# Attention on one core: the own weights u·r·k as stationary columns beside another tile's logits, and a matmul with ones in place of a transposition

## The chip, the core and the metric

The kernel runs on one core of a Trainium2 chip. The metric is the device time of one execution in microseconds (us), as a median over runs. The core has a matrix engine (TensorE, PE in the rows, with PEld for its weight loads), VectorE (DVE), ScalarE (ACT), GpSimd (POOL), and SyncE (SP), which issues most DMA transfers. TensorE multiplies a stationary operand, which is loaded into its array column by column, with a moving operand that streams through; results go to PSUM. A matmul with fp32 operands is issued as two passes, each with a weight load of its own, so four such matmuls stand in a row as x8.

## The reference

A linear attention over 768 steps (batch 4, 8 heads of width 48) feeds two mixture-of-experts layers. Only the attention and the logits of the first gate matter here:

```
for t in range(S):
    cur = einsum('bhd,bhe->bhde', u * kt, vt)
    y[:, :, t] = einsum('bhd,bhde->bhe', rt, state + cur)
    state = w * state + einsum('bhd,bhe->bhde', kt, vt)
...
x = y.transpose(0, 2, 1, 3).reshape(B * S, H * D)      # 3072 tokens of width 384
logits = x @ w_gate ; eom = sigmoid(x @ w_output_gate)
```

The term with `cur` gives a token its own value: for each head, y gets (sum over d of u·r·k) times v. This one number for each token and head is called its own weight here.

## The kernel before

The tokens are cut into 24 tiles of 128 (6 chunks of time for 4 batches). A loop over t = 0 to 23 runs the attention as a pipeline: in iteration t each step works on the tile that it is ready for. The order in which the instructions of TensorE, VectorE and ScalarE stand is the order of the code, written out by hand; each engine works through its list in order. The steps, by their names in the code and in the rows:

- `s_rk` (VectorE): `rks`, r and k of tile t+1 times powers of w. `s_pr` (GpSimd): `rkp`, the product r·k of tile t+1. `s_kn` (GpSimd): `kn`.
- `s_a` (TensorE): `a`, the products of r and k inside tile t, 8 matmuls; `s_am` (VectorE) masks them into `am`. Two PSUM banks hold `a`, so the next tile's `a` needs this tile's `am`.
- `s_t` (TensorE): 4 transpositions of tile t-2's output into the bank `t`. `s_csm` (TensorE) puts the own weights of tile t into spare columns of that bank: 4 matmuls with `rkp` stationary (128 columns) and `usel` moving (two columns, u of the two heads of a pair). In the first two iterations there is no `s_t`, and the bank is called `c`.
- `s_cs` (VectorE) copies the own weights out as `cs`; `s_cv` (ScalarE) multiplies v by them, 8 small activations, `cv`, one iteration later; `s_x` (VectorE) adds `cv` to the transposed output: `x`.
- `s_y` (TensorE): `y` of tile t-1, from the state (`st`) and from `am`; `s_yt` (ScalarE) copies it out.
- `s_l` (TensorE): the logits of tile t-4, 3 matmuls with the gate's weights `wg_s` stationary (32 columns) and the transposed tokens `xth` moving. Each of the three parts of the width 384 goes into a group of 32 PSUM partitions of its own in the bank `sp`; the fourth group is unused. `s_s` puts the update of the state into the same bank.
- `s_xt` (TensorE) and `s_xh` (ScalarE): transposition of the tokens of tile t-3 into `xth`.
- `s_ls` (ScalarE) copies the 96 partitions of logits out, `s_lt` (TensorE) transposes them into the bank `lg` of their group of tiles, and `s_r1` (VectorE) adds the three parts and starts the routing; `s_r2`, `s_r3`, `s_r4` finish it, and GpSimd scatters the tokens to their experts (`xs`). For the last groups a matmul with `fold` (ones that add the three parts) takes the place of the transposition already.

After the loop a hand-written tail finishes tiles 20 to 23. In its last steps six scatters run on GpSimd, one behind the other. Then 26 warm-up matmuls run on TensorE, and the first expert stage begins with loads of the scattered tokens (`xe<-xs`).

At the start `usel` is made by two copies on VectorE. In iteration 2 a check of w (`s_flag`) computes `okr` on VectorE and a matmul of it on TensorE.

## Time and profile before

| what | value |
|---|---|
| median of 3 runs | 1927.33 us (1926.3 to 1927.76) |
| the profiled execution's own time | 1927.44 us |
| its span, from the first to the last instruction | 1925.4 us |
| TensorE busy over the span | 98% |
| VectorE, ScalarE, GpSimd busy | 70%, 43%, 24% |
| granted TensorE clock, mean | 0.987 |
| iteration 4 of the attention loop begins | 42.59 us |
| its tail begins | 160.34 us |

The times in the rows count from the first instruction of the span. A busy TensorE is one that has a matmul under way; matmuls overlap, so what a step costs is read from the start of its first matmul to the start of the next step's first matmul. The clock is given as a share of its upper level of 2.4 GHz; 0.50 is the lower level of 1.2 GHz.

### The profile page before, as it was taken

The page shows a single profiled execution, that of the slowest core. Times are in us where ns is not written, and L with a number is a line of the kernel's source. Part 1 is how long each engine was busy: PE and PEld are TensorE (multiplying, and loading weights), DVE is VectorE, ACT ScalarE, POOL GpSimd, SP SyncE. Part 2 cuts the span into 40 slices and gives each one's busy share as a digit, 9 for nine tenths or more (in the row PEclk, how much of TensorE's full clock was granted, in tenths as well). Part 3 has the DMA queues.
Part 4 walks back from the last instruction along what each step waited for, and adds up shares of the span by engine and source line. Part 5 has one row for each costly group of instructions (what it writes and reads, how often), then busy time and mean ns, then how long its engine had stood idle before and what let it go on. Part 6 is the DMA issues. An engine that isn't in the chain of part 4 may idle for free.

```text
span 1925.4 us, 27928 instructions
## 1 busy us (share of the span) xinstructions
PE 1890.4 (98%) x10851; PEld 1715.8 (89%) x10852; DVE 1347.9 (70%) x2296; ACT 834.2 (43%) x1687; POOL 471.0 (24%) x507
## 2 busy tenths in 40 slices
PE   8998999999999999999999999999999999999998
PEld 6886999977989999999999888999999999999997
DVE  6885555666887677777777787567777777667774
ACT  2664444444444444434444444543443444444432
POOL 4673000211213322221111344122111111111112
PEclk7998999999999999999999999999999999999999
DMA  7764444221111111111111112111111111111101
GB/s 223 238 209 127 139 129 135 73 59 34 34 34 34 33 34 34 34 41 41 34 33 34 33 33 78 38 34 34 33 39 37 34 33 37 39 33 34 33 25 49
DMA packets 43916, 118.39 MB, mean 61 GB/s; under 512 B 6737, under 2 KB 10065, under 8 KB 43777
## 3 DMA queue, kind: packets, MB, share of 16 engines
q1 hardware_dynamic: 38944, 107.04, 19.4%
q0 software_dynamic: 3904, 9.47, 1.4%
q8 instruction: 86, 1.41, 0.3%
q14 instruction: 54, 0.43, 0.1%
q10 hardware_dynamic: 928, 0.04, 0.0%
HBM read 101.96 MB, written 14.56 MB: 61 GB/s over the span
## 4 chain that ended last, share of the span: by engine, by line
PE 73%; DVE 2%; issue 2%; POOL 1%; ACT 0%; POOLq 0%; DVEq 0%
PE o L1217 39%; PE bS L1170 13%; PE bT L1170 11%; PE bZ L1170 4%; PE bW L1170 4%; POOL out L1237 1%; DVE wal L875 1%; POOL ws L846 1%; DVE hc L1183 0%; PE lgp L1097 0%; DVE hl L1204 0%; DVE slot L925 0%; DVE x L1235 0%; ACT hc L1180 0%; PE pcp L1146 0%
## 5 line engine op out<-in xcount | busy, mean ns | idle before, releaser
L1217 PE MATMUL o<-wbh,hl 128*128 128x384 f32 x1536 | 518.6, 338 | 0.4 <-DVE hl L1204 0.3
L1217 PE MATMUL o<-wbl,hh 128*128 128x384 f32 x1536 | 518.5, 338 | 0.0
L1217 PE MATMUL o<-wbh,hh 128*128 128x384 f32 x1536 | 517.5, 337 | 0.7 <-DVE x L1229 0.3
L846 POOL TENSOR_TENSOR ws<-ra 128x384 f32<-128x384 f32 (+2 forms) x192 | 195.0, 1044 | 1093.1 <-DVE wal L875 1013.6
L1204 DVE SCALAR_TENSOR_TENSOR hl<-hc,hh 128x512 fp32r<-128x512 f32 x384 | 278.3, 727 | 206.7 <-ACT hh L1203 201.1
L1217 PEld LDWEIGHTS o<-wbh,hh 128*128 128x128 f32 x1536 | 289.1, 188 | 42.7 <-DVE x L1235 1.1
L1217 PEld LDWEIGHTS o<-wbh,hl 128*128 128x128 f32 x1536 | 288.3, 188 | 43.1 <-DVE hl L1204 1.3
L1217 PEld LDWEIGHTS o<-wbl,hh 128*128 128x128 f32 x1536 | 288.5, 188 | 0.0
L1180 ACT COPY hc<-bT 128x512 f32<-128x512 f32 x192 | 113.0, 588 | 400.4 <-PE bT L1170 398.6
L1180 ACT COPY hc<-bS 128x512 f32<-128x512 f32 x192 | 112.9, 588 | 370.8 <-PE bS L1170 370.7
L1203 ACT ACTIVATE hh<-hc 128x512 fp32r<-128x512 f32 x384 | 240.1, 633 | 11.7 <-PE o L1217 11.7
L1170 PE MATMUL bS<-slot,wah 128*128 128x512 f32 x704 | 226.0, 394 | 8.7 <-DVE hc L1183 6.6
L1235 DVE SCALAR_TENSOR_TENSOR x<-o,pw,x 128x384 f32<-128x384 f32 x348 | 204.9, 610 | 22.3 <-PE o L1217 17.9
L1170 PE MATMUL bT<-slot,wah 128*128 128x512 f32 x640 | 201.1, 396 | 0.0
L1183 DVE TENSOR_TENSOR hc<-bS,hc 128x512 f32<-128x512 f32 x192 | 132.2, 688 | 43.2 <-PE bS L1170 41.6
L1170 PE MATMUL bS<-slot,wal 128*128 128x512 f32 x384 | 151.6, 395 | 0.0
L1170 PEld LDWEIGHTS bS<-slot,wah 128*128 128x128 f32 x704 | 128.5, 188 | 15.3 <-DVE hc L1183 9.7
L875 DVE TENSOR_TENSOR wal<-ws,wah 128x384 fp32r<-128x384 f32 (+2 forms) x192 | 133.1, 693 | 9.3 <-ACT wah L874 9.2
L1170 PE MATMUL bT<-slot,wal 128*128 128x512 f32 x320 | 126.3, 395 | 0.0
L1183 DVE TENSOR_TENSOR hc<-bT,hc 128x512 f32<-128x512 f32 x128 | 87.9, 687 | 52.5 <-PE bT L1170 49.8
L874 ACT CAST wah<-ws 128x384 fp32r<-128x384 f32 (+2 forms) x192 | 117.6, 612 | 3.0 <-POOL ws L846 3.0
L1170 PEld LDWEIGHTS bT<-slot,wah 128*128 128x128 f32 x640 | 116.5, 188 | 2.4 <-DVE hc L1189 0.8
(235 smaller groups left out, 2705.1 us busy)
## 6 DMA issues: line engine op xcount, KB each, us to landing
raw<-in_wm SPq DMA_DIRECT2D x64, 384.0 KB
ra<-in_wm SPq DMA_DIRECT2D x64, 384.0 KB
rb<-in_wm SPq DMA_DIRECT2D x64, 384.0 KB
rk<-in_rkt SPq DMA_DIRECT2D x25, 448.0 KB
na<-in_nat SPq DMA_DIRECT2D x25, 384.0 KB
xs<-zer SPq DMA_DIRECT2D x8, 624.0 KB
xe<-xs SPq DMA_DIRECT2D x8, 624.0 KB
xs<-x,posl POOLq DMA_INDIRECT x24
```

The costliest lines, as they stand in the source:

```text
L846: gsum.append(tc.keep_in_program_order(nc.gpsimd.tensor_tensor(*x)))
L874: nc.scalar.copy(hi[:, q], x)
L875: nc.vector.tensor_tensor(lo[:, q], x, hi[:, q].bitcast(F32), ALU.subtract)
L1170: nc.tensor.matmul(bank[bk], w_[:, at, :], x_, start=(opens == 1 and n == 0), stop=(n == 2), skip_group_check=True)
L1180: A.copy(hid(u, *copy[p]), ps)
L1183: V.tensor_tensor(h, ps, h, ALU.add)
L1203: A.activation(hh, h, AF.Relu)
L1204: V.scalar_tensor_tensor(hl, h, 0.0, hh.bitcast(F32), ALU.max, ALU.subtract)
L1217: nc.tensor.matmul(ob[j], h_[:, j * P:(j + 1) * P], w_[:, c], start=(f == 0 and m == 0), stop=(f == 3 and m == 2))
L1235: V.scalar_tensor_tensor(acc, ob[j], wt, acc, ALU.mult, ALU.add)
L1237: s = nc.gpsimd.indirect_dma_start(out=out, out_offset=bass.IndirectOffsetOnAxis(ap=toks[:, i:i + 1].bitcast(U32), axis=0), in_=acc, in_of ...
```

## The change

- `s_csm` is gone. The own weights are made inside `s_l`: `usel`, now 32 columns wide with u of head h in column h, is stationary, `rkp` moves. The 4 matmuls go into the partition groups 2 and 3 of the bank, two into each, the second adding to the first; the logits of tile t-4 take groups 0 and 1 (the first and the third part add up in group 0). In iterations 0 to 3, where no tile has logits yet, the logit matmuls run on `ident`.
- `s_ls` copies 128 partitions. `s_lt` is a matmul with `fold` for all tiles: it turns the logits and adds the parts, for logits (16 columns) and own weights (8 columns) at once, and now runs from iteration 1 on. The reduction that added the parts in `s_r1` is gone.
- `s_cs` reads the own weights from `lg`, two iterations after `s_l`, at the beginning of the iteration; `s_cv` follows in that iteration. `s_x` of the same tile stands in the same iteration too. `na`, which holds v, has 6 buffers for 5.
- `usel` is filled by 8 small copies on GpSimd; `fold` is made by two additions on VectorE.
- In the tail, `s_lt(19)`, `s_cs(22)`, `s_cv(22)`, `s_cs(23)` and `s_cvd(23)` stand at its beginning.

```
-        nc.vector.tensor_reduce(fold, ident[:LW, :LW].rearrange("q (k e) -> q e k", k=KD)[:, 0:2 * E], AX.X, ALU.add)
+        nc.vector.tensor_tensor(fold[:, 0:2 * E], ident[:, 0:2 * E], ident[:, 32:32 + 2 * E], ALU.add)
+        nc.vector.tensor_tensor(fold[:, 2 * E:], ident[:, 64:64 + H], ident[:, 96:96 + H], ALU.add)
...
-        usel = acst.tile([112, 4, 2], F32, name="usel")
+        usel = acst.tile([112, 4, 32], F32, name="usel")
...
-            na = ain.tile([P, 2, D], F32, name=f"na{i}", tag="na", bufs=5)
+            na = ain.tile([P, 2, D], F32, name=f"na{i}", tag="na", bufs=6)
...
-                nc.vector.tensor_copy(usel[o:o + HD, :, par], uc[o:o + HD, :])
+                nc.gpsimd.tensor_copy(usel[o:o + HD, p, h:h + 1], uc[o:o + HD, p:p + 1])
...
-        def s_csm(i, bank):
-            rkp[i, "bank"] = bank
-            for p in range(4):
-                nc.tensor.matmul(bank[:, 448 + 2 * p:450 + 2 * p], rkp[i][:, p, :], usel[:, p, :], start=True, stop=True,
-                                 skip_group_check=True)
...
-            nc.vector.tensor_copy(wk[i]["cs"], rkp[i, "bank"][:, 448:456])
+            nc.vector.tensor_copy(wk[i]["cs"], groups[g][:, j * LF + 2 * E:(j + 1) * LF])
...
-            for k in range(KD):
-                nc.tensor.matmul(lp[4 * E * k:4 * E * (k + 1)], wg1_s[:, k, :], wk[i]["xh"][:, k, :], start=True,
-                                 stop=True, skip_group_check=True)
+            xh = [wk[i]["xh"][:, k, :] for k in range(KD)] if i >= 0 else [ident] * KD
+            logit = lambda q, k, first: nc.tensor.matmul(
+                lp[32 * q:32 * (q + 1)], wg1_s[:, k, :], xh[k], start=first, stop=True, skip_group_check=True)
+            own = lambda q, p, first: nc.tensor.matmul(
+                lp[32 * q:32 * (q + 1)], usel[:, p, :], rkp[i + 4][:, p, :], start=first, stop=True,
+                skip_group_check=True)
+            both = i + 4 < NT
+            logit(0, 0, True)
+            if both:
+                own(2, 0, True)
+            logit(1, 1, True)
+            if both:
+                own(3, 1, True)
+            logit(0, 2, False)
+            if both:
+                own(2, 2, False)
+                own(3, 3, False)
...
-            if g < GT:
-                nc.tensor.transpose(groups[g][:, j * LW:(j + 1) * LW], wk[i]["ls"], ident[:LW, :LW])
...
+            nc.tensor.matmul(groups[g][:, j * LF:j * LF + w], lsof[i], fold[:n, :w], start=True, stop=True,
+                             skip_group_check=True)
...
-                if on(1):
-                    s_cv(t - 1)
+                if on(2):
+                    s_cs(t - 2)
+                    s_cv(t - 2)
...
-                s_csm(t, s_t(t - 2) if on(2) else aps.tile([P, 512], F32, name=f"c{t}", tag="t", bufs=2))
+                if on(2):
+                    s_t(t - 2)
...
-                s_cs(t)
...
-                if on(4):
-                    s_l(t - 4, sp_)
+                s_l(t - 4, sp_)
...
-                if on(5):
+                if t > 0:
                     s_lt(t - 5)
...
+            s_lt(19)
+            s_cs(22)
+            s_cv(22)
+            s_cs(23)
             s_cvd(23)
...
-            s_lt(19)
             todo += s_r1(6)
```

Where the instructions stand: TensorE in iteration 9, from the end of `a` to the beginning of `y`. Before:

```order
L303 MATMUL a9_1_932<-rks9_860 128x128
L303 MATMUL a9_0_931<-rks9_860 128x128
L303 MATMUL a9_1_932<-rks9_860 128x128
L364 MATMUL t7_955<-ident_80,yt7_893 128x112 x4
L276 MATMUL t7_955<-usel_128,rkp9_840 128x2 x4
L325 MATMUL y8_976<-rks8_768,st0_145 64x128
```

With the change:

```order
L300 MATMUL a9_0_947<-rks9_875 128x128
L300 MATMUL a9_1_948<-rks9_875 128x128
L361 MATMUL t7_973<-ident_80,yt7_910 128x112 x4
L322 MATMUL y8_988<-rks8_783,st0_145 64x128
L322 MATMUL y8_988<-rks8_783,st0_145 48x128
```

The four matmuls of the own weights, which stood between the transpositions and `y`, are gone from here.

TensorE in the same iteration, from the end of `y` to the update of the state. Before:

```order
L331 MATMUL y8_976<-am8_0_862,na8_548 64x128
L331 MATMUL y8_976<-am8_1_864,na8_548 48x128
L396 MATMUL sp9_975<-xth5_912,wg1_s_100 32x128 x3
L344 MATMUL sp9_975<-na8_548,kn8_838 64x48
L344 MATMUL sp9_975<-na8_548,kn8_838 48x48
```

With the change:

```order
L328 MATMUL y8_988<-am8_1_879,na8_565 48x128
L394 MATMUL sp9_987<-xth5_929,wg1_s_100 32x128
L396 MATMUL sp9_987<-rkp9_857,usel_128 32x128
L394 MATMUL sp9_987<-xth5_929,wg1_s_100 32x128
L396 MATMUL sp9_987<-rkp9_857,usel_128 32x128
L394 MATMUL sp9_987<-xth5_929,wg1_s_100 32x128
L396 MATMUL sp9_987<-rkp9_857,usel_128 32x128 x2
L341 MATMUL sp9_987<-na8_565,kn8_855 64x48
```

Three matmuls of 32 stationary columns have become seven, logits of tile 5 and own weights of tile 9 in turn.

ScalarE at the beginning of the tail. Before:

```order
L401 COPY ls19_2452<-sp23_2418 96x128
L387 COPY xth20_2454<-xt20_2448 128x384
L505 ACTIVATE x16_1926<-x16_1926,g5_2465 128x384
L505 ACTIVATE x17_2032<-x17_2032,g5_2465 128x384
L337 COPY yt23_2506<-y23_2480 112x512
```

With the change:

```order
L414 COPY ls19_2457<-sp23_2420 128x128
L384 COPY xth20_2459<-xt20_2453 128x384
L284 ACTIVATE cv22_2476<-na22_1967,cs22_2474 128x48 x8
L515 ACTIVATE x16_1933<-x16_1933,g5_2470 128x384
L515 ACTIVATE x17_2038<-x17_2038,g5_2470 128x384
L334 COPY yt23_2524<-y23_2499 112x512
```

The 8 activations of `cv22` now stand between `xth20` and the copy of tile 23's output.

## Rows read from the trace of the kernel before

**Rows 1.** Busy time by stretch, iteration 10; (x) counts instructions:

```profile
core 0: us, PE busy (x) PEld busy (x) DVE busy (x) ACT busy (x) POOL busy (x), PEclk, DMA share, GB/s
77.59:83.56 5.97, 5.97 (x87) 5.09 (x87) 5.64 (x13) 2.98 (x11) 5.21 (x8) 1.00 0.73 209
```

**Rows 2.** Timeline of PE, iteration 15: start us, us to the end, instructions:

```profile
107.65 1.16 PE L303 MATMUL a<-rks 48*128 48x128 f32 x16
108.75 0.60 PE L364 MATMUL t<-ident,yt 112*128 112x112 f32 x4
109.19 0.96 PE L276 MATMUL t<-usel,rkp 112*128 112x2 f32 x8
110.08 1.08 PE L325 MATMUL y<-rks,st 48*64 48x128 f32 x16
111.09 1.09 PE L331 MATMUL y<-am,na 128*64 128x128 f32 x16
112.11 0.42 PE L396 MATMUL sp<-xth,wg_s 128*32 128x128 f32 x6
112.46 0.67 PE L344 MATMUL sp<-na,kn 128*64 128x48 f32 x16
...
113.62 1.16 PE L303 MATMUL a<-rks 48*128 48x128 f32 x16
```

**Rows 3.** Timeline of PE at 112.15 and at 112.45, inside the logits:

```profile
112.11 0.31 PE L396 MATMUL sp<-xth,wg_s 128*32 128x128 f32 x3
...
112.25 0.29 PE L396 MATMUL sp<-xth,wg_s 128*32 128x128 f32 x3
```

**Rows 4.** Timeline of PE, both forms of the last step before the same follower:

```profile
101.27 0.25 PE L411 MATMUL lg<-ident,ls 96*128 96x96 f32 x1
...
101.36 0.19 PE L461 MATMUL lg<-o_all,maskb 128*128 128x64 bf16 x1
...
159.94 0.29 PE L413 MATMUL lg<-fold,ls 96*128 96x16 f32 x2
160.09 0.18 PE L461 MATMUL lg<-o_all,maskb 128*128 128x32 bf16 x1
```

**Rows 5.** Busy time by stretch, columns as in Rows 1, at the slow clock:

```profile
33.78:42.59 8.81, 8.81 (x67) 7.68 (x66) 4.53 (x8) 2.28 (x9) 2.94 (x3) 0.50 0.55 171
15.50:42.70 27.20, 24.87 (x189) 22.07 (x189) 13.83 (x27) 7.29 (x28) 9.31 (x8) 0.50 0.70 223
```

**Rows 6.** Timeline of PE at the start; in brackets idle time before, and what ended it:

```profile
14.03 1.02 PE L276 MATMUL c<-usel,rkp 112*128 112x2 f32 x8 [1.86 <-DVE usel L246]
...
30.94 0.19 PE L529 MATMUL sp<-okr,onesf 112*1 112x1 f32 x2 [2.03 <-DVE okr L528]
...
37.37 1.73 PE L276 MATMUL t<-usel,rkp 112*128 112x2 f32 x8
39.03 1.97 PE L331 MATMUL y<-am,na 128*64 128x128 f32 x16
```

**Rows 7.** Timeline of POOL and DVE at the start:

```profile
6.09 1.27 POOL L268 TENSOR_TENSOR rkp<-rk 112x512 f32<-112x512 f32 x1 [1.58 <-DMA rk<-in_rkt]
...
12.75 1.13 DVE L246 COPY usel<-uc 48x4 f32<-48x4 f32 x2
...
29.00 0.17 DVE L281 COPY cs<-t 128x8 f32<-128x8 f32 x1 [1.97 <-issue]
```

**Rows 8.** Timeline of ACT and POOL, iteration 23 and the tail:

```profile
155.53 1.92 ACT L287 ACTIVATE cv<-na,cs 128x48 f32<-128x48 f32 x8
...
160.47 0.48 ACT L387 COPY xth<-xt 128x384 f32<-128x384 f32 x1
161.44 1.12 ACT L505 ACTIVATE x<-x,g 128x384 f32<-128x384 f32 x2 [0.49 <-DVE g L494]
163.03 0.59 ACT L337 COPY yt<-y 112x512 f32<-112x512 f32 x1 [0.47 <-PE y L331]
...
167.72 0.97 POOL L506 DMA_INDIRECT xs<-x,posl  x1 [3.13 <-DVE r L448]
```

More of the change, by code (lines that the diff above doesn't have):

```diff
@@ L42 @@
 GT = 6
-LW = 4 * E * KD
+LF = 2 * E + 8
 CONV = (7, 8, 11, 12, 15, 16)
@@ L156, in linattn_moe_moe2_kernel @@
     c_run = const.tile([P, GT + 1, E], BF16, name="c_run")
-    fold = const.tile([LW, 2 * E], F32, name="fold")
+    fold = const.tile([P, LF], F32, name="fold")
     nc.vector.memset(c_run[:, 0, :], 0.0)
@@ L243, in linattn_moe_moe2_kernel @@
         small_consts()
-        for par in range(2):
-            o = par * 64
-            nc.vector.tensor_copy(usel[o:o + HD, :, par], uc[o:o + HD, :])
+        for p in range(4):
+            for par in range(2):
+                o, h = par * 64, 2 * p + par
+                nc.gpsimd.tensor_copy(usel[o:o + HD, p, h:h + 1], uc[o:o + HD, p:p + 1])
         todo = []
@@ L389, in lcol @@
         def lcol(sp_, i):
[L390 removed]
+            return sp_(i) if callable(sp_) else sp_[:, 256:256 + P]
         def s_l(i, sp_):
             lp = lcol(sp_, i)
[L395 to L402 removed]
+            xh = [wk[i]["xh"][:, k, :] for k in range(KD)] if i >= 0 else [ident] * KD
@@ L404, in linattn_moe_moe2_kernel, with lgof @@
+            if both:
[4 more added lines that the diff above has]
+                own(3, 3, False)
+        def s_ls(i, sp_):
+            n = P if i + 4 < NT else 64
+            ls = awk.tile([P, P], F32, name=f"ls{i}", tag="ls")
+            nc.scalar.copy(ls[:n], lcol(sp_, i)[:n])
+            lsof[i] = ls[:n]
+        lsof = {}
         gof = {i0 + j: (g, j, n) for g, (i0, n) in enumerate(GROUPS) for j in range(n)}
+        def lgof(i):
+            return gof[i][:2] if i >= 0 else (-1, i + 4)
@@ L406, in s_lt @@
         def s_lt(i):
-            g, j, n = gof[i]
+            g, j = lgof(i)
             if j == 0:
-                groups[g] = aps.tile([P, 512], F32, name=f"lg{g}", tag="m", bufs=2)
-            if g < GT:
-                nc.tensor.transpose(groups[g][:, j * LW:(j + 1) * LW], wk[i]["ls"], ident[:LW, :LW])
-            else:
-                nc.tensor.matmul(groups[g][:, j * 2 * E:(j + 1) * 2 * E], wk[i]["ls"], fold, start=True, stop=True,
-                                 skip_group_check=True)
+                groups[g] = aps.tile([P, 512], F32, name=f"lg{max(g, 0)}_{i < 0}", tag="m", bufs=2)
@@ L423, in s_r1 @@
             i0, n = GROUPS[c]
-            lg = groups[c][:, 0:n * 2 * E].rearrange("t (b e) -> t b e", b=n)
+            lg = groups[c][:, 0:n * LF].rearrange("t (b e) -> t b e", b=n)[:, :, 0:2 * E]
             o = o_all[:, i0:i0 + n, :]
@@ L430, in s_r1 @@
             V = nc.vector
-            first = []
-            if c < GT:
-                parts = groups[c][:, 0:n * LW].rearrange("t (b k s e) -> t b s e k", b=n, k=KD, s=2)[:, :, 0]
-                lg = rtile(c, "lg", [P, n, 2 * E])
-                first = [lambda: V.tensor_reduce(lg, parts, AX.X, ALU.add)]
             def zsum():
@@ L440, in zsum @@
                 nc.scalar.activation(ez, zr, AF.Exp, scale=-1.0)
-            return first + [
+            return [
                 lambda: V.tensor_reduce(mx, lg[:, :, 0:E], AX.X, ALU.max),
```

14 lines of the change are left out of this document (6 added, 8 removed).

## Prediction

> **What bounds the kernel now.** I began with the busy time by stretch, because a share over the whole span mixes stages. In iteration 10 TensorE is busy for 5.97 us of 5.97 us [rows 1], and iterations 5 to 20 all last as long, a little longer where a group's routing adds its matmuls. VectorE, the next, has 5.64 us of work in this its fullest iteration [rows 1]. So I read TensorE in order of time next. In iteration 15 each step begins as soon as the array lets it, with no wait: from `a` to the next `a` 113.62 - 107.65 = 5.97 us [rows 2]. What shortens this list shortens the stage, as long as no other engine takes over. The first iterations are another case: TensorE's clock is at 0.50 from 15.5 to 42.7 us [rows 5], and TensorE waits for VectorE twice, 1.86 us for `usel` and 2.03 us for `okr` [rows 6]. The tail is a third: a chain of short steps over all engines, read by who waits for whom [rows 8].
>
> **What goes from an iteration.** Between the first transposition (108.75) and `y` (110.08) lie 1.33 us [rows 2]. The 4 transpositions take 0.60 us from the first start to the last end, and one such, that of `lg`, lasts 0.25 us [rows 4], so the last starts about 0.35 us after the first. From there to the first matmul of a step that cuts the array otherwise it takes about 0.2 us: from the second round of the logits at 112.25 to the next step at 112.46 it is 0.21 [rows 2, 3]. Without the own weights `y` would start 0.35 + 0.20 = 0.55 us after the first transposition instead of 1.33. Saved: 0.78 us.
>
> **What comes in.** Seven matmuls of two passes each in the logits' place, where three stood. The rows show how such passes go: three start together at 112.11, one in each group of 32 columns, the second three at 112.25, and the whole step takes 112.46 - 112.11 = 0.35 us [rows 2, 3]. So passes in different groups run side by side, and a round costs what one pass streams. For the length of a round I take `y`: 16 passes, two side by side, in 1.01 us, of which 0.2 are the change of step: about 0.11 us for each round [rows 2]. With the change the groups have 4, 2, 4 and 4 passes, so 4 rounds instead of 2: +2 x 0.11 = +0.22 us. It can hardly be less, since the passes of one group follow each other; with rounds of 0.14, as the first (112.11 to 112.25), it is 0.28. From above: all 14 passes one behind the other, 12 more rounds, +1.32 us. I take 0.22, the row being of the same step with the same shapes, three groups of four.
>
> The last step becomes a matmul of two passes for a transposition of one. Before the same follower the one takes 101.36 - 101.27 = 0.09 us, the other 160.09 - 159.94 = 0.15 [rows 4]: +0.06; where its second weight load isn't hidden, another pass of 128 stationary columns costs what the own weights cost, 8 in about 0.9 us [rows 2], +0.11. I take +0.10.
>
> Sum for an iteration: -0.78 + 0.22 + 0.10 = **-0.46 us**, between -0.39 (0.28 and 0.11) and -0.50 (0.22 and 0.06). The 20 iterations 4 to 23 give **-9.2 us** (-7.8 to -10.0).
>
> **What is costed at nothing.** `cs` moves to the beginning of VectorE's iteration and waits for the last matmul of the iteration before, which is over by then; VectorE does the same copy, and the reduction of the three parts falls away. `cv` then starts some tenths later in an iteration and is wanted in the same one by `x`; that stands on VectorE behind both `am`, and its 1.92 us [rows 8] end before. If they don't, `x` is late, but the transposition that reads it comes an iteration later. The eight `usel` copies run on GpSimd while it waits for the first `rk` (1.58 us idle [rows 7]); beyond that they would delay `kn`, for which nobody waits. The sixth `na` buffer keeps v for the later `cv`, so loads go out no later.
>
> **The start.** Three things. The `usel` copies leave VectorE's list, 1.13 us [rows 7]; `rks` and `am` behind them come that much earlier, less 0.1 for the second addition of `fold`: -1.0 us. In iteration 2 `cs` no longer makes VectorE wait for TensorE (1.97 us idle [rows 7]) ahead of `okr`, for which TensorE then waits 2.03 us [rows 6]: -2.0 us. In iterations 1 to 3 at half the clock the own weights cost 39.03 - 37.37 = 1.66 us [rows 6], less 0.2 for the change of step; the four rounds that come in whole there cost 4 x 0.22 + 0.2 = 1.1 us and the new last step about 0.4: nothing is won. That makes -3.0 us at an unchanged clock. The clock itself: it fell after TensorE had waited at 14.03 with little behind it, and rose at about 42.7, after TensorE had run on without a wait from 30.94, through `y`, `sp` and the whole iteration 3 [rows 5, 6]. With the wait for `okr` gone or short that unbroken run begins earlier, and rounds that stream stand where weights were loaded for two columns. I count a rise 3 us earlier, a third of iteration 3's 8.81 us [rows 5]; at the full clock that work takes half as long: -1.5. Together **-4.5 us**; at worst -2 (the waits go only in part and the clock rises as before), at best -8 (the rise comes an iteration or two earlier).
>
> **The tail.** `cv22`, 1.92 us, now stands between `xth` (160.47, ends 160.95) and the two scalings (1.12 us); tile 23's copy `yt` can't start before 160.95 + 1.92 + 1.12 = 163.99, against 163.03, when it waited 0.47 us for `y` [rows 8]. Behind `yt` on TensorE stand tile 23's transpositions and the routing of group 6, whose scatter GpSimd awaits for 3.13 us at 167.72 [rows 8]; five more scatters queue behind it. So **+0.9 us**. The four tail logits take 4 rounds each for 2, +0.2 each; the first is hidden behind `yt`, the others lie ahead of the last scatters, which GpSimd's queue holds back anyway. Bounds 0 and +1.6. After that the expert stage starts as it did, only earlier; where its first matmuls fall in a slow stretch of the clock may shift, which I allow 1.5 us both ways.
>
> **Sum.** -9.2 - 4.5 + 0.9 = -12.8. From the profiled execution's 1927.44 us (span 1925.4 and 2.0 around it; the median of the runs is 1927.33, 0.1 less) that gives 1914.6 us. With every bound at its worst: -7.8 - 2.0 + 1.6 + 1.5 = -6.7, 1920.7; at its best -10.0 - 8.0 - 1.5 = -19.5, 1907.9.
>
> **Rivals.**
> 1. The passes start strictly in the order of the list, so that a matmul's second pass, which waits for its first, holds back the next group. The seven matmuls, in turn over the groups, then take 8 rounds: 6 more, +0.66, and an iteration changes by -0.78 + 0.66 + 0.10 = -0.02 us, the 20 by -0.4. With the start at about -0.4 (three half-rate iterations with 4 further rounds of 0.22 take 2.6 of the 3.0 back) and the tail +0.9 the time is 1927.5: no change. Against it: the three logits before would then have started at two, not three, in a round; all three first passes started together [rows 3]. The Trainium skill, "TensorE: Matmul & The Clock Gate", Part 3 (packing small matmuls), says that matmuls start and end strictly in program order, with no reordering. By that rule this rival's 1927.5 us would come out; the rows on the logits disagree with it across column groups. 6 in 100.
> 2. Slower: the own weights and the logits, read from different tiles with 112 and 128 rows, don't overlap at all. 14 rounds, +1.32, so +0.64 us an iteration, +12.8; the tail +0.9; at the start ten further rounds of 0.22 in three iterations (+6.6) against -3.0: 1927.4 + 17.3 = 1944.7 us. It decides from (0.78 - 0.10) / 0.11 = 6.2 further rounds on, so with more than 8 rounds in all. No row shows two such operands side by side; for the overlap speaks that three moving operands did [rows 3]. 5 in 100.
> 3. VectorE becomes the bound. It has 5.64 us in iteration 10 [rows 1], where TensorE would want 5.51. If it paces iterations 9 to 23, each wins 0.33 instead of 0.46: 15 x 0.13 = 2.0 us less, 1916.6 us. For it speaks how close the two are; against it that iteration 10 is the fullest and that VectorE may fall behind by the time for which `a` waits on no one. 11 in 100.
>
> The forecast has 78 in 100.
>
> **How the numbers follow.** 1914.6 us is the forecast's. 1908 to 1921 takes in its bounds and the third rival and leaves out the first two, 11 in 100, and a little of the ends. A measurement of this kernel can tell about 0.2% (3.9 us) from no change; faster than that are the forecast and the third rival, 0.89; within it the first, 0.06; slower the second, 0.05.
>
> **What would show it.** In the changed profile: iterations of about 5.5 us between the starts of `a`, with VectorE near full; `y` about 0.55 us after the first transposition; the seven matmuls about 0.57 us from their start to the state's update; the first three iterations shorter, with the clock at 0.50 for less than 27 us; `yt` of tile 23 late by about 1 us against the tail's beginning. The prediction is wrong if the step of seven takes 1 us or more, if TensorE shows waits for VectorE's `am` in iterations 9 to 23, or if the slow clock lasts longer than before.

## The result and the profile after

The changed kernel takes 1906.22 us in the median of 4 runs (1903.52 to 1909.59), the kernel before 1926.82 (1925.63 to 1927.76) beside it: a ratio of 0.9896 (95% interval 0.9883 to 0.991), 20.6 us less. The forecast was 1914.6 with a range of 1908 to 1921; the time lies 1.8 us under the range. The profiled execution took 1905.73 us, its span 1903.7. Where its 21.7 us come from, by the first rows of each part in the two timelines:

| stretch | before | after | difference | forecast |
|---|---|---|---|---|
| start to `a` of iteration 4 | 42.59 | 34.35 | -8.24 | -4.5 |
| iterations 4 to 22 (19) | 112.16 | 102.21 | -9.95 | -8.7 |
| `a` of iteration 23 to the last scatter | 19.48 | 19.73 | +0.25 | +0.4 (-0.46 + 0.9) |
| last scatter to the expert stage's first `bS` | 241.33 | 240.53 | -0.80 | 0 |
| expert stage, to the end of the span | 1509.84 | 1506.88 | -2.96 | 0 |

**The loop.** Timeline of PE in the changed kernel, iteration 15, which answers to [rows 2, 3]:

```profile
93.66 1.16 PE L300 MATMUL a<-rks 48*128 48x128 f32 x16
94.75 0.60 PE L361 MATMUL t<-ident,yt 112*128 112x112 f32 x4
95.28 1.08 PE L322 MATMUL y<-rks,st 48*64 48x128 f32 x16
...
97.31 0.30 PE L394 MATMUL sp<-xth,wg_s 128*32 128x128 f32 x1
97.32 0.30 PE L396 MATMUL sp<-rkp,usel 112*32 112x128 f32 x1
97.33 0.30 PE L394 MATMUL sp<-xth,wg_s 128*32 128x128 f32 x1
97.33 0.30 PE L396 MATMUL sp<-rkp,usel 112*32 112x128 f32 x1
97.44 0.27 PE L394 MATMUL sp<-xth,wg_s 128*32 128x128 f32 x1
...
97.66 0.27 PE L394 MATMUL sp<-xth,wg_s 128*32 128x128 f32 x1
97.67 0.29 PE L396 MATMUL sp<-rkp,usel 112*32 112x128 f32 x2
97.89 0.67 PE L341 MATMUL sp<-na,kn 128*64 128x48 f32 x16
...
98.86 0.30 PE L429 MATMUL lg_False<-fold,ls 128*128 128x24 f32 x2
99.09 0.38 PE L300 MATMUL a<-rks 48*128 48x128 f32 x2
```

From `a` to `a` 5.43 us, 0.54 less than in [rows 2]. `y` follows the first transposition after 0.53 us instead of 1.33. Four first passes, one in each group of columns, start within 0.02 us; the further rounds begin at 97.44, 97.55 and 97.66, and the next step at 97.89, 0.58 after the first pass. The last step, with `fold`, takes 0.23 us up to the next `a`, where the transposition took 0.18.

Busy time by stretch, columns as in Rows 1, which answer to [rows 1, 5]: iterations 10 and 15, the two stretches of the start at half the clock, and the whole start from the first `a` to that of iteration 4:

```profile
66.22:71.66 5.44, 5.44 (x89) 4.54 (x88) 4.70 (x13) 3.34 (x13) 4.41 (x4) 1.00 0.74 220
93.66:99.09 5.43, 5.43 (x88) 4.54 (x87) 5.15 (x7) 4.49 (x14) 3.70 (x5) 1.00 0.63 173
12.00:18.80 6.80, 5.75 (x43) 3.78 (x44) 2.42 (x4) 0.27 (x1) 6.49 (x7) 0.50 0.80 213
25.70:29.00 3.30, 3.30 (x45) 2.55 (x42) 0.64 (x3) 0.58 (x1) 0.52 (x1) 0.50 0.98 296
10.58:34.35 23.77, 19.87 (x240) 15.15 (x243) 14.07 (x31) 6.67 (x24) 14.63 (x14) 0.78 0.92 283
```

In iteration 10 VectorE has 4.70 us in 5.44 and is further from the bound than before; in iteration 15, now its fullest, it has 5.15 in 5.43. TensorE has no wait above 0.15 us from iteration 4 to the end of iteration 22, so VectorE doesn't pace the loop. The slow clock lasts about 10 us in two pieces (12.0 to 18.8 and 25.65 to 29.06), where it lasted 27 in one [rows 5].

**The start.** Timelines of PE, of POOL (the eight copies together, then two of them by themselves) and of DVE there, which answer to [rows 6, 7]; in brackets idle time before, and what ended it:

```profile
13.72 0.42 PE L396 MATMUL sp<-rkp,usel 112*32 112x128 f32 x1 [0.72 <-POOL rkp L270]
...
25.36 0.19 PE L539 MATMUL sp<-okr,onesf 112*1 112x1 f32 x2 [2.53 <-DVE okr L538]
```

```profile
8.30 4.01 POOL L248 COPY usel<-uc 48x1 f32<-48x1 f32 x8 [3.69 <-DMA uc<-in_ucol]
...
9.40 1.30 POOL L248 COPY usel<-uc 48x1 f32<-48x1 f32 x1
...
10.99 1.32 POOL L248 COPY usel<-uc 48x1 f32<-48x1 f32 x1
12.40 1.27 POOL L270 TENSOR_TENSOR rkp<-rk 112x512 f32<-112x512 f32 x1
```

```profile
10.66 0.15 DVE L142 CAST rev<-revi 128x8 f32<-128x8 int32 x1
...
11.06 1.21 DVE L258 TENSOR_TENSOR rks<-rk,tab 112x1024 f32<-112x1024 f32 x1
...
25.05 0.16 DVE L538 TENSOR_REDUCE okr<-oka 112x1 f32<-112x4 f32 x1
```

Not as forecast: TensorE's wait for `okr`, which was to go, is longer (2.53 for 2.03 us). `cs` no longer holds VectorE up, and VectorE reaches `okr` at 25.05 instead of 30.64. But the own weights, 1.73 us of TensorE's work ahead of the matmul on `okr` in iteration 2 of the kernel before, are gone too, and TensorE, which has its full clock there now (18.82 to 25.65), reaches that matmul at 22.83 instead of 28.91. The eight `usel` copies take 4.01 us after a wait for their DMA, `rkp` of tile 0 comes at 12.40 instead of 6.09 [rows 7], and TensorE waits for it. Six of the eight take 0.18 to 0.21 us each; the two shown take 1.30 and 1.32 and end 0.2 us or less behind VectorE's two `rks` (9.30 to 10.52 and 11.06 to 12.27), beside which they run.

**The tail.** Timeline of ACT, which answers to [rows 8]:

```profile
142.22 1.91 ACT L284 ACTIVATE cv<-na,cs 128x48 f32<-128x48 f32 x8 [0.31 <-DVE cs L278]
144.04 1.11 ACT L515 ACTIVATE x<-x,g 128x384 f32<-128x384 f32 x2
145.06 0.56 ACT L334 COPY yt<-y 112x512 f32<-112x512 f32 x1
```

`yt` of tile 23 starts without idle time, 8.50 us behind `a` of iteration 23 (136.56); before 163.03 - 154.75 = 8.28.

### The profile page after: what moved, and what is told of

Its sections match the earlier page's. It is cut to its first block, busy times and chain, and to the rows that moved or that the text cites. A ratio compares the mean times of both kernels' runs of the same rounds, so it can differ in the third digit from the quotient of the medians.

```text
span 1903.7 us, 28040 instructions
## 1 busy us (share of the span) xinstructions
PE 1869.9 (98%) x10896; PEld 1689.6 (89%) x10902; DVE 1337.0 (70%) x2289; ACT 834.7 (44%) x1691; POOL 473.4 (25%) x515
## 4 chain that ended last, share of the span: by engine, by line
PE 75%; DVE 2%; issue 1%; POOL 1%; ACT 0%; POOLq 0%; DVEq 0%
PE o L1229 40%; PE bS L1182 14%; PE bT L1182 11%; PE bZ L1182 5%; PE bW L1182 4%; DVE wal L887 1%; DVE hc L1195 1%; POOL out L1249 0%; DVE x L1247 0%; PE lgp L1109 0%; POOL ws L858 0%; DVE slot L937 0%; DVE hl L1216 0%; ACT hh L1215 0%; PE pcp L1158 0%
```

## Experiments

Eighteen runs followed, of sixteen new kernels; a_again is the changed kernel a second time, a_both2_again the kernel of a_both2. The names say what was changed: b_ is built on the kernel before, a_ on the changed one. "Start" is the time of the first `a` of iteration 4, "loop" from there to that of iteration 23, "expert" from the first `bS` to the span's end, in the profiled execution; the ratio is to the kernel before, run beside it.

| kernel | start | loop | expert | ratio (95%) |
|---|---|---|---|---|
| before | 42.59 | 112.16 | 1509.9 | |
| after | 34.35 | 102.21 | 1506.9 | 0.9896 (0.9883 to 0.991) |
| a_again | 36.35 | 102.21 | 1505.8 | 0.9901 (0.9881 to 0.9922) |
| a_dup1 | 36.53 | 102.34 | 1505.8 | 0.991 (0.9881 to 0.9939) |
| a_dup3 | 33.02 | 106.39 | 1505.8 | 0.9923 (0.9893 to 0.9953) |
| a_seq | 32.18 | 102.47 | 1506.6 | 0.9908 (0.9879 to 0.9938) |
| b_ok_early | 33.29 | 112.10 | 1508.9 | 0.9969 (0.9955 to 0.9983) |
| b_usel_pool | 39.95 | 112.52 | 1510.0 | 0.9984 (0.9973 to 0.9995) |
| a_ok_early | 30.16 | 102.23 | 1506.9 | 0.9896 (0.9871 to 0.992) |
| a_usel_act | 33.59 | 102.21 | 1506.7 | 0.9897 (0.987 to 0.9923) |
| a_both | 30.61 | 145.42 | 1505.8 | 1.0118 (1.009 to 1.0146) |
| a_both2 | 30.15 | 102.23 | 1505.9 | 0.9877 (0.9862 to 0.9893) |
| a_both2_again | 30.12 | 102.23 | 1505.9 | 0.9879 (0.9858 to 0.99) |
| a_warm | 29.72 | 102.23 | 1506.8 | 0.9878 (0.9862 to 0.9894) |
| a_na5 | 34.26 | 106.64 | 1505.8 | 0.9908 (0.9892 to 0.9923) |
| b_fold24 | 39.54 | 112.08 | 1506.9 | 0.9986 (0.9969 to 1.0002) |
| a_fold32 | 36.15 | 102.21 | 1511.8 | 0.9927 (0.9913 to 0.994) |
| a_both2_p0 | 32.08 | 102.22 | 1508.9 | 0.9892 (0.9876 to 0.9909) |
| a_both2_m32 | 32.47 | 102.21 | 1508.9 | 0.9874 (0.9857 to 0.989) |
| a_both2_m64 | 32.48 | 102.23 | 1513.8 | 0.9902 (0.9885 to 0.9918) |

Two things are read from the table by themselves. The start differs by 4 us between kernels whose edits touch it little or not at all (after, a_again, a_dup1, a_seq and a_fold32: 32.2 to 36.5); a_again, the same kernel as after, differs from it by 2.0. And the clock falls to 0.50 for 3.4 us once in the expert stage of some executions and not of others (the fall at its very end, which all have, aside), which costs it about 1 us (b_ok_early 1508.9 without, before 1509.9 with one fall; a_again 1505.8 without, after 1506.9 with one; a_both2_m32 and a_both2_m64 had two).

### What a round costs: a_dup1, a_dup3, a_seq

```diff
 # a_dup1
             logit(1, 1, True)
+            logit(1, 1, True)
 # a_dup3
                 own(3, 1, True)
+                own(3, 1, True)
 # a_seq: the order of the calls
+logit(0, 0), logit(0, 2), logit(1, 1), own(2, 0), own(2, 2), own(3, 1), own(3, 3)
```

> The changed kernel with the matmul of the second logit (group 1, the group with one matmul for the others' two) issued twice in a row; the second overwrites the first, so the output is the same. Theory of rounds (passes in different groups of 32 columns run side by side, so only the fullest group counts): group 1 then has 4 passes like the others, and an iteration stays at 5.44 us, within 0.03. Rival (passes cost their number, or start strictly in the list's order): two further passes at 0.11 make 5.66. Whole time within 2 us of the changed kernel's by the first; 5 us more by the second.

> The changed kernel with the first own-weight matmul of group 3, which is among the full groups, issued twice in a row; the output is the same. Theory of rounds: group 3 has 6 passes, so two more rounds of 0.11 us, and an iteration takes 5.64 to 5.68 us instead of 5.44; over 20 iterations 4.0 to 4.8 us, with the first iterations about 5.5 us on the whole. Rival (the repeated matmul fills gaps): 5.44. Rival (one behind the other for all): also 5.66, but then the run with the repeated logit shows it too.

> The changed kernel with the seven matmuls in another order, one group of columns after another (both logits of group 0, the one of group 1, both own-weight matmuls of group 2, both of group 3) instead of in turn over the groups. Theory that each group of columns takes its passes whenever it is free: still 4 rounds, an iteration at 5.44 us. Theory that a pass can't start before the one ahead of it in the list has started: a pass that waits for its own group holds back the others; counted by hand 11 rounds instead of 4, +0.77 us, an iteration of about 6.2 us, and the whole time 15 to 19 us more, slower than the changed kernel by far and close to the kernel before.

Timeline of PE in the loop of a_dup1, the first pass and the next step:

```profile
72.09 0.30 PE L394 MATMUL sp<-xth,wg_s 128*32 128x128 f32 x1
...
72.67 0.67 PE L341 MATMUL sp<-na,kn 128*64 128x48 f32 x16
```

The same of a_dup3:

```profile
75.52 0.30 PE L394 MATMUL sp<-xth,wg_s 128*32 128x128 f32 x1
...
76.31 0.67 PE L341 MATMUL sp<-na,kn 128*64 128x48 f32 x16
```

And of a_seq, with its last round:

```profile
73.24 0.31 PE L394 MATMUL sp<-xth,wg_s 128*32 128x128 f32 x2
73.26 0.31 PE L396 MATMUL sp<-rkp,usel 112*32 112x128 f32 x2
...
73.61 0.29 PE L396 MATMUL sp<-rkp,usel 112*32 112x128 f32 x2
73.83 0.67 PE L341 MATMUL sp<-na,kn 128*64 128x48 f32 x16
```

From the first pass to the next step: 0.58 us with two more passes in the free group, 0.79 with two more in a full one, 0.59 in the order of a_seq. Over 19 iterations the loop grew by 0.13, 4.18 (0.22 an iteration, two rounds) and 0.26 us. In these runs only the fullest group counts, and the order of the list does not. In a_seq two passes of the own weights start at 73.26, when only two of the six logit passes that stand ahead of them in the list have started. This refutes the first rival also in the order that should have hurt most. The Trainium skill, "TensorE: Matmul & The Clock Gate", Part 3, has matmuls start and end strictly in program order; across groups of columns the rows of a_seq disagree, and the measurement decides.

### The start: b_ok_early, a_ok_early, b_usel_pool, a_usel_act

```diff
 # b_ok_early, a_ok_early
                 s_am(t)
+                if t == 0:
+                    s_ok()      # the four VectorE operations that end in okr
 # b_usel_pool (two copies), a_usel_act (eight)
-            nc.vector.tensor_copy(usel[o:o + HD, :, par], uc[o:o + HD, :])
+            nc.gpsimd.tensor_copy(usel[o:o + HD, :, par], uc[o:o + HD, :])
-                nc.gpsimd.tensor_copy(usel[o:o + HD, p, h:h + 1], uc[o:o + HD, p:p + 1])
+                nc.scalar.copy(usel[o:o + HD, p, h:h + 1], uc[o:o + HD, p:p + 1])
```

> The kernel before, with the four small VectorE operations that end in `okr` moved from iteration 2 to the end of iteration 0, where VectorE waits for `rk`; the matmul on `okr` stays where it is. The kernel before showed TensorE waiting 2.03 us for `okr`, with the clock at 0.50 from 15.5 to 42.7 us and iteration 4's `a` at 42.59. Theory 1 (a wait is worth its own length): that wait goes, the slow stretch keeps its end against the work, and `a` of iteration 4 starts at 40.6, 2.0 earlier. Theory 2 (the wait's larger price is the clock, which rises only after TensorE has run on for some time): the unbroken run begins a whole iteration earlier, the clock rises one iteration earlier and `a` of iteration 4 starts at 36 to 38.5, 4 to 6.5 us earlier. Rival: TensorE then waits at the next place as long, and nothing is won (42.6). The whole time falls by as much as `a`.

Timeline of PE and busy time by stretch of b_ok_early:

```profile
26.94 0.19 PE L532 MATMUL sp<-okr,onesf 112*1 112x1 f32 x2
...
33.29 0.94 PE L303 MATMUL a<-rks 48*128 48x128 f32 x12
```

```profile
11.09:24.75 13.66, 12.29 (x87) 10.72 (x88) 10.11 (x19) 3.79 (x16) 8.08 (x7) 0.50 0.91 286
```

A wait of 2.03 us, taken from the kernel before by moving four operations of VectorE, brings the start to 33.29: 9.3 us earlier than in the kernel before, 6.3 earlier than in the other profile of that start (b_fold24, 39.54). The clock comes back at 24.75 instead of 42.7 and stays up. By the timed runs it is 6.0 us (3.3 to 8.7), about three times the wait, so theory 1's price is too low and theory 2 has the right kind (its 36 to 38.5 was too late). Its reason is shown in part. The clock rose at 24.75, ahead of the matmul on `okr` (26.94), so that rise can't come from the missing wait; what is missing with it is the slow stretch behind the matmul. In all nine profiles without the wait (those with the `okr` move) none follows before iteration 4. Of the eleven with it, eight have the clock at 0.50 behind it; a_dup3, a_seq and a_fold32, which waited 2.77, 2.02 and 2.31 us, do not. So a slow stretch behind the wait is frequent and not certain.

> The changed kernel with the same move of the four operations on `okr` to iteration 0. There TensorE waited 2.53 us for `okr` at 25.36, the clock fell to 0.50 at 25.65 and rose at 29.07, and `a` of iteration 4 started at 34.35. Theory 1 (the wait alone): `a` of iteration 4 at 31.8. Theory 2 (the clock's fall belongs to the wait): the clock stays up, the 3.4 us at half of it take 1.7, and `a` starts at 30.0 to 30.3; the time falls by 4.2 us. Rival: TensorE waits for another producer of iteration 2 instead, and less than 1 us is won.

Busy time by stretch of a_ok_early, the start at the lower clock and the rest of it:

```profile
11.87:18.70 6.83, 5.89 (x43) 3.69 (x44) 5.75 (x8) 0.27 (x1) 6.75 (x7) 0.50 0.92 252
18.70:30.16 11.46, 11.14 (x185) 9.14 (x184) 8.90 (x18) 6.41 (x23) 7.42 (x6) 1.00 1.01 300
```

The start is 30.16, as theory 2 had it; the fall at 25.65 is gone. The median of its four runs was 1905.46, which doesn't tell it from the changed kernel; what this move alone is worth there in time is not shown. a_both2 below, with a second move beside it, is told apart.

> The kernel before, with the two `usel` copies moved from VectorE's list to GpSimd's, as the change moves its eight; nothing else. The forecast's price for this was 1.0 us of the start, at an unchanged clock. Theory 1 (the list alone): `rks` of tile 1 starts 1.1 us earlier (12.8 instead of 13.91), TensorE's 1.86 us at `c` shrink by that, and `a` of iteration 4 starts 1 us earlier than the 39.5 to 42.6 of the two profiles with that start so far. Theory 2 (GpSimd's `rkp` and `kn` come later, so that VectorE's casts of `rev` and `qf` run alone): they take 0.15 and 0.23 instead of 0.97 and 1.26, and `rks` of tile 1 starts near 11.1. By both, TensorE's wait for `okr` in iteration 2 stays, and with it most of the slow stretch: `a` of iteration 4 at 37 to 41.5. Rival: without the wait at `c` the clock comes back early as it did without the wait for `okr`: `a` of iteration 4 at 33 to 35.

Timeline of PE and busy time by stretch of b_usel_pool:

```profile
28.30 0.19 PE L529 MATMUL sp<-okr,onesf 112*1 112x1 f32 x2 [2.03 <-DVE okr L528]
```

```profile
10.13:23.78 13.65, 12.42 (x90) 11.12 (x92) 8.14 (x16) 3.61 (x16) 10.52 (x8) 0.50 0.91 283
27.20:40.85 13.65, 12.55 (x107) 11.33 (x109) 7.05 (x15) 3.77 (x13) 3.73 (x4) 0.50 0.58 172
```

The start is 39.95, between the two starts of that order without the edit (42.59 and 39.54); by the timed runs the edit wins 3.1 us (1.0 to 5.2). The wait for `okr` stays, and the clock, back at 23.78, falls again at 27.20. So the copies' place is worth some 3 us (1.0 to 5.2) and not the 8. `rks` of tile 1 started at 12.59: theory 1's number, though not by its reason, since `rkp` now stood beside `rks` of tile 0 and made that 2.11 us long.

> The changed kernel with the eight `usel` copies on ScalarE instead of GpSimd. GpSimd's list at the start is then that of the kernel before: `rkp` of tile 0 at about 6.1 instead of 12.40, with `rkp` of tile 1 and two `kn` from 10.4 to 13.7, beside VectorE's small casts. Theory A (a VectorE cast of a few numbers takes about 1 us while GpSimd has a two-input operation running): the casts of `rev` and `qf` take about 1.0 and 1.3 us again, where they took 0.15 and 0.23, and `rks` of tile 1 starts at 12.7 to 13.1 instead of 11.06. Theory B (the casts were short for another reason, such as the changed operation between them): they stay at 0.15 and 0.23 and `rks` of tile 1 at 11.1. By both, TensorE's wait for `rkp` (0.72 us) goes; by A one for `rks` takes its place. Whole time within 2 us of the changed kernel's.

Timelines of DVE and of POOL in a_usel_act:

```profile
10.66 0.96 DVE L142 CAST rev<-revi 128x8 f32<-128x8 int32 x1
11.55 0.15 DVE L143 TENSOR_TENSOR fold<-ident 128x16 f32<-128x16 f32 x1
11.63 1.23 DVE L144 TENSOR_TENSOR fold<-ident 128x8 f32<-128x8 f32 x1
```

```profile
10.57 1.03 POOL L264 TENSOR_TENSOR kn<-na,tabn 128x384 f32<-128x384 f32 x1 [3.40 <-ACT tabn L236]
11.57 1.27 POOL L270 TENSOR_TENSOR rkp<-rk 112x512 f32<-112x512 f32 x1
```

Theory A, with a correction: what is held up is a small operation that meets GpSimd's, here `rev` and the second addition of `fold` (0.15 us each in the changed kernel), not `qf`. The eight copies in the changed kernel show it the other way round: two of them were held up beside VectorE's `rks`. `rev` ends at 11.62 and `kn` at 11.60; the addition ends at 12.86 and `rkp` at 12.84. The Trainium skill, "SBUF — State Buffer", section "SBUF: two separate sides", says that VectorE and GpSimd share a port which one instruction holds to its end; these ends agree. `rks` of tile 1 starts at 12.95 instead of 11.06, and the start is no later (33.59): both are covered by the landing of `rk` of tile 2, for which VectorE waits until 17.17 here and 17.85 there.

### A mistake, and the start without its waits: a_both, a_both2, a_warm

```diff
 # a_both2: a_ok_early, and behind s_pr(0) in iteration 0
                 if t == 0:
                     s_pr(0)
+                    for p in range(4):
+                        for par in range(2):
+                            o, h = par * 64, 2 * p + par
+                            nc.gpsimd.tensor_copy(usel[o:o + HD, p, h:h + 1], uc[o:o + HD, p:p + 1])
 # a_warm: a_both2 and fillers
-            warm_up(15, wps)
+            warm_up(26, wps)
...
-                    warm_up(2, wps)
+                    warm_up(14 if t == 1 else 2, wps)
```

> The changed kernel with two moves: the operations on `okr` in iteration 0, and on GpSimd the eight `usel` copies behind `rkp` of tile 0 instead of ahead of it. Expected beside the run with the `okr` move alone: `rkp` of tile 0 at 6.1 to 7.4, `usel` ready at 12.3 as before, so that TensorE's 0.72 us for `rkp` go. Theory 1 (waits alone): `a` of iteration 1 0.7 us earlier, `a` of iteration 2 held by the landing of its `rk` (17.85) and its `rks` at no earlier than 19.1, so `a` of iteration 4 0.7 us earlier than with one move. Theory 2 (clock): with the wait gone the clock falls later or not at all, and 1 to 2.5 us are won on one move alone. Rival: all of it is hidden behind the landing of `rk`, 0. Time of the kernel: about 1901 by the first and 1899.5 by the second.

The kernel was not what this says: the copies stood outside the `if` and ran in every iteration. Waits of PE in a_both from 60 to 180 us (us in total, times, longest), and one iteration by stretch:

```profile
PE sp L392 <- POOL usel L570: 12.5, 8, 2.5
```

```profile
86.22:98.29 12.07, 11.41 (x95) 8.45 (x94) 4.24 (x13) 4.21 (x15) 6.49 (x13) 0.52 0.54 186
```

The copies made the loop 43.2 us longer. Eight waits of TensorE are 12.5 us of it, and the clock stood at 0.50 for 41 us of the loop; the iteration shown, in which TensorE was busy for 11.41 of 12.07 us, went at 0.52. Here too the slow clock goes with the waits, but not each of the eight has a fall behind it, and how the 43.2 us divide is not shown, since the copies also hold up GpSimd's other work.

> The changed kernel with the operations on `okr` in iteration 0 and the eight `usel` copies, once, behind `rkp` of tile 0 on GpSimd. (In the run labelled a_both those copies were written into the body of the loop by mistake and ran in each of the 24 iterations.) `rkp` of tile 0 at 6.1 to 7.4 us, `usel` ready at 12.3. Theory 1 (waits alone): `a` of iteration 1 0.7 us earlier than with the `okr` move alone (14.0), `a` of iteration 2 no earlier than 19.1, `a` of iteration 4 at 29.5. Theory 2 (clock): with the wait at 13.7 gone the clock falls later or for a shorter time, `a` of iteration 4 at 28.5 to 30. Rival: hidden behind the landing of `rk` of tile 2, 30.2 as with one move. Time 1 to 5 us under the changed kernel's.

The start is 30.15, not earlier than with one move (30.16): in these two profiles the rival held. The medians, 1901.75 here and 1905.46 with one move, each from four runs and not beside each other, leave open whether the second move helps in other executions.

> The kernel of a_both2 with 26 further filler matmuls on TensorE (the kind that the kernel already issues ahead of its first tile) where TensorE would stand idle in the first 20 us: 11 behind the first 15, 3 behind the transpositions of `tab`, 12 in iteration 1 while `rk` of tile 2 is on its way. They compute nothing that is used. Theory that the clock falls after TensorE has stood idle and that this is the larger part of the start's price: the clock stays at its upper level until the tail, `a` of iteration 4 starts at 28 to 29, and that time no longer differs between executions. Theory that the clock at the start falls whatever TensorE does: `a` of iteration 4 at 30 or later, since the fillers also stand in the way. Rival: the fillers end later than what they fill and cost more than they bring, 31.

Busy time by stretch of a_warm, the whole start:

```profile
10.58:29.72 19.14, 18.66 (x253) 13.79 (x256) 15.62 (x31) 6.67 (x24) 14.76 (x15) 1.00 0.94 297
```

The clock stays at 1.00, as the first theory says, but the start gains only 0.4 us more than a_both2: what the lower clock still cost there, from 10.35 to 17.18, lay beside the landing of `rk` of tile 2, for which VectorE waits until 17.24 here. The number expected, 28 to 29, was too early.

> The changed kernel as it is, a second time. Its profile so far had `a` of iteration 4 at 34.35 and 1506.9 us of expert stage; five kernels with the same start had 32.2 to 36.5. Theory: the start differs by some 4 us between executions of one kernel, by how long the clock stays at its lower level, while the loop (5.44 us an iteration) and the expert stage (1505.5 to 1507) don't. Expected 1903 to 1909, with `a` of iteration 4 between 32 and 37. Rival: the first profile was a lucky one, and the start lies at 37 or later.

> The kernel of a_both2 a second time, on the chip and beside the runs on which the changed kernel is run again, for the difference of the two. By its one profile it wins 4.2 us ahead of iteration 4 (30.15 for 34.35) and nothing behind; by the medians of separate calls 4.5 us. Expected: 3 to 5 us under the changed kernel's median. Rival: the changed kernel's own spread covers it, and the two differ by less than 2 us.

The changed kernel took 1906.48 us (1902.11 to 1909.51), a_both2 1901.86 (1899.78 to 1902.71): 4.6 less, as expected, for the two moves together. No version here is told apart as faster: a_warm took 1901.81 beside a_both2's 1901.75, and a_both2_m32 has the ratio 0.9874. In a_again the clock was at 0.50 for 17.1 us of the start (10.07 to 20.32, 27.14 to 33.97) where the first profile had 10, and its start is 2.0 us later.

### The sixth buffer: a_na5

```diff
-            na = ain.tile([P, 2, D], F32, name=f"na{i}", tag="na", bufs=6)
+            na = ain.tile([P, 2, D], F32, name=f"na{i}", tag="na", bufs=5)
```

> The changed kernel with five `na` buffers, as before the change, instead of six. The forecast costed the sixth buffer at nothing: it keeps v for the later `cv`, so that loads go out no later. Theory that the sixth is needed for that: the load of tile t+3 waits for `cv` of an earlier tile, a loop iteration stays at 5.44 us as long as the loads land in time, and the time stays within 2 us of the changed kernel's, unless a load is late, which would show as TensorE waiting for `kn` or `y` waiting for `na`, 0.3 us or more in each iteration (6 us and more in all). Rival: the sixth buffer itself brings part of the gain, and the iterations are longer by a few hundredths each.

Waits of SP's DMA queue in a_na5, 40 to 100 us, and of PE from 70 to 93:

```profile
SPq L188 <- ACT cv L284: 19.3, 6, 4.5
```

```profile
PE t L361 <- DVE x L371: 3.6, 2, 2.1
```

The loop is 4.4 us longer, all of it in iterations 11 to 13 (6.14, 6.99 and 7.85 us for 5.44, 5.44 and 5.68). SP's queue stands still until `cv` lets a buffer go, and `x` on VectorE then stands behind two splits of expert weights (L113) of 3.3 us each, which take 0.95 in the changed kernel. That the late loads are what moved and stretched these splits is read from the order of the rows and not tested. The sixth buffer is what makes the later `cv` free. In every other iteration five would do.

### The expert stage: b_fold24, a_fold32, a_both2_p0, a_both2_m32, a_both2_m64

```diff
 # b_fold24 (+32 bytes against the kernel before)
-    fold = const.tile([LW, 2 * E], F32, name="fold")
+    fold24 = const.tile([LW, 24], F32, name="fold")
+    fold = fold24[:, 0:2 * E]
 # a_fold32 (+64): 32 columns, the first 24 used
 # a_both2_p0 (0), _m32 (-32), _m64 (-64): fold in another pool, spare constants of 64, 32 and 0 bytes
+    spare = const.tile([P, 16], F32, name="spare")
```

> The kernel before, with one edit that adds no work: the constant tile `fold` is 24 columns wide instead of 16, of which the last 8 are never used, so that every tile placed behind it lies 32 bytes further on, as in the changed kernel. In the changed kernel each repetition of the expert stage's pattern (about 46 us) came out 0.107 us shorter than in the kernel before, in each execution profiled so far, with no wait and no instruction changed. Theory of the place (where the tiles lie in the partition sets a nanosecond or two of single matmuls): the expert stage is 2.5 to 3.5 us shorter than in the kernel before, everything ahead of it as before, the time 1924 to 1925. Theory of the instructions' place (the stream of TensorE's instructions in front is longer by a hundred): no change in the expert stage, 1927. Rival: only executions differ, either way by chance.

> The changed kernel with its constant tile `fold` 32 columns wide instead of 24, the last 8 never used: every tile placed behind it lies another 32 bytes further on, 64 beyond the kernel before. No work is added. Theory that the place of the expert stage's tiles counts in steps of 64 bytes: the expert stage, 1506.9 us from its first `bS` to the end in the changed kernel and 1509.9 in the kernel before, is back at 1509 to 1510, and the time 3 us more than the changed kernel's, about 1909. Rival (any place but that of the kernel before will do, or it is the number of instructions ahead): it stays at 1506 to 1507.

> The kernel of a_both2 with the tile `fold` taken from the constants into the pool that ends with the attention, and 64 bytes of unused constants in its stead: the expert stage's tiles lie where they lay in the kernel before, while all else of the change stays. Theory of the place: the expert stage, 1505.9 us in a_both2, is back at 1508 to 1510, as in the kernel before. Rival (another part of the change made the expert stage shorter): 1505 to 1507.

> As a_both2_p0, with 32 bytes of unused constants: the expert stage's tiles lie 32 bytes ahead of those of the kernel before. Measured so far against the kernel before: 32 bytes behind, 0.107 us less in each repetition of 46 us; 64 bytes behind, 0.066 more. Theory that only the remainder by 64 bytes counts is refuted already, since 0 and 64 differ. Theory that the remainder by 128 counts: this is a place not yet seen (as 96), and any rate between those two or beyond may come out. Theory that the only good places are odd multiples of 32: as in a_both2, 1505 to 1507.

> As a_both2_p0, without any unused constants: the expert stage's tiles lie 64 bytes ahead of those of the kernel before. Theory that the remainder by 128 bytes counts: as in a_fold32, where they lay 64 bytes behind, 1511 to 1512 us for the expert stage. Theory that they are the better the further ahead: below 1505. Rival: as in the kernel before, 1508 to 1510.

Groups of instructions of PE from 700 to 1100 us, the same matmul in the kernel before, in the changed one and in a_fold32 (count, busy us, mean ns):

```profile
L1217 PE MATMUL o<-wbl,hh 128*128 128x384 f32 x416 | 140.4, 337 | 0.0
```

```profile
L1229 PE MATMUL o<-wbl,hh 128*128 128x384 f32 x416 | 139.6, 335 | 0.0
```

```profile
L1230 PE MATMUL o<-wbl,hh 128*128 128x384 f32 x416 | 141.0, 339 | 0.0
```

TensorE's waits in these 400 us are 0.6, 1.1 and 0.6 us in all, so they don't make the difference; the same matmuls are a nanosecond or two shorter or longer. Set beside the kernel before by the starts of `bS`, a repetition of about 46 us is shorter by 0.107 us in b_fold24 (+32 bytes), as in the changed kernel; unchanged, to the hundredth, in a_both2_p0 (0); longer by 0.066 in a_fold32 (+64); shorter by 0.080 in a_both2_m32 (-32); longer by 0.080 in a_both2_m64 (-64). So the whole 3.0 us of the expert stage come from the 32 bytes by which the wider `fold` moves what lies behind it. The theory of steps of 64 bytes fell, since -64, 0 and +64 differ, and so did that of the remainder by 128, as the 0.066 and 0.080 of +64 and -64 are not the same; both odd multiples of 32 that ran are good. By what rule, and which of the tiles it is, stays open.

## Why the prediction was wrong, point by point

The time came out under the range because of a term that stood at nothing, the expert stage (-3.0 us), together with one that was too small, the start (-8.2 us for -4.5 in the profiled pair). With either of them as forecast the time would have been 1909 or 1910, in the range.

- **The loop: right.** Saved 0.80 us for 0.78 an iteration, four rounds for +0.23 (0.22), the last step +0.05 for +0.10, under its lower bound of +0.06: -0.52 for -0.46, just past the better bound of -0.50, and -9.95 us for -8.7 over 19 iterations. The one step mis-sized was the price of `fold`'s second weight load, of which the rows show nothing.
- **The rivals.** Strict order (first) and no overlap (second) fell by a_seq, a_dup1 and a_dup3. VectorE as the bound (third) fell since TensorE shows no wait in the loop, though VectorE comes as near as 5.15 us in 5.43.
- **The start: the term that was mis-sized.** The forecast's step was that `cs` no longer holds up `okr` (-2.0), and that the clock rises 3 us earlier (-1.5). The first went only half way: VectorE came to `okr` 5.6 us earlier (25.05), but TensorE, at the full clock and without the own weights in its list, came to it 6.1 us earlier and waited 2.53 us. The second was far larger: 10 and 17 us at the lower clock in two executions instead of 27 (24 in b_fold24). -4.5 became -8.2 in the profiled pair; over the starts seen (42.59 and 39.54 before, 32.2 to 36.5 in the changed kernel and those of its start) it is about 6 us. That taking away a single wait of 2 us there is worth 6 us is shown (b_ok_early), and that no slow stretch then follows it; which part of the change brought the clock back at 18.8 us, though the wait stayed, is not: the `usel` copies alone did not (b_usel_pool), and the forecast's reason, rounds that stream where weights were loaded, is argued only.
- **`usel` costed at nothing: wrong in the reason.** The copies were not done while GpSimd waited for `rk`; they waited for `uc` themselves, took 4.01 us, 2.6 of them in two copies beside VectorE's `rks`, and held up `rkp`. That cost little, since `rk` of tile 2 comes no earlier (a_both2), and gave VectorE's small operations a free stretch.
- **The sixth buffer: right,** and worth 4.4 us in the profile of a_na5.
- **The tail: right in size.** +0.25 us from `a` of iteration 23 to the last scatter for the forecast's +0.44. Between there and the expert stage the kernels of the table lie 240.2 to 241.6 us apart from scatter to `bS`, so the -0.8 there is spread.
- **The expert stage: the step that failed.** "The expert stage starts as it did, only earlier" left out that a constant grown by 32 bytes moves every later tile: -3.0 us (b_fold24, a_both2_p0). The 1.5 us that the forecast allowed here were for the clock; for this no bound was kept. In the profiled pair the parts beyond the forecast are 3.7 (start), 3.0 (expert stage), 1.2 (loop), 0.8 and 0.2 (behind the last scatter and in the tail): 8.9 of 21.7 us.

## What to carry to other kernels

Price a wait of TensorE by the clock around it and not by its length alone: where the profile showed 0.50 behind a wait of 2 us, moving four small operations to an earlier idle stretch was worth 6 us, beside 10 us from the shorter step of 19 iterations. Small matmuls in different groups of 32 columns cost here as many rounds as the fullest group had passes, in both orders tried, so an empty group was free. When a tile changes its size, compare a stage that was not touched: a shift of 32 bytes moved 1500 us of matmuls by 3 us, and a spare constant can undo or copy that.

## What was not expected of the hardware

- The rate of TensorE's matmuls depended on where the tiles of their stage lie: 1505.8, 1508.9 and 1511.8 us (the last with one fall of the clock) for the same stage at +32, 0 and +64 bytes.
- Two VectorE operations on a few numbers that met a two-input operation of GpSimd ended when that ended: 0.96 and 1.23 us for 0.15. It goes the other way too: GpSimd's copies of 48x1 took 0.18 to 0.21 us, and 1.30 and 1.32 beside a two-input operation of VectorE.
